# A transformer block on one core: its plan rebuilt with a longer time for the row sums' trip to DRAM, and the normalised h transposed by a DMA

## The chip, the cores and the metric

The kernel runs on one core of one Trainium2 chip. The metric is device time in microseconds (us), as the median of several executions. Engines are named as the profile names them: PE is TensorE (matmuls), PEld its weight loads, DVE is VectorE, ACT is ScalarE, POOL is GpSimd, SPq is the DMA queue that SyncE feeds.

## The reference

x has 2048 tokens of width 1024. There are 32 heads of width 32 that share one key and one value, and a feed-forward part of width 3584. All arrays are bf16.

```python
h  = x + attention(layernorm(x)) @ wo           # softmax over all 2048 keys
h2 = h + (sigmoid(n @ w_gate) * (n @ w_up)) @ w_down,   n = layernorm(h)
```

## The kernel before

The kernel is a small scheduler. It walks through the work once on the host with a formula for the duration of each operation, writes an ordered list of instructions for each engine, and then emits the lists with semaphore waits. The formula never runs on the chip: it only decides the order. Each engine then executes its list in that order, so an operation whose input is late holds up what is listed behind it: in the first trip shown below DVE stood idle 3.29 us before one multiplication, and the additions and the eviction listed behind it began only after it.

The formula for a DMA, in the planner's step:

```python
go = max(s + 1300.0, self.dma_free)
self.dma_free = go + o.nbytes / self.DMA_RATE      # DMA_RATE = 260 bytes per ns
o.end = self.dma_free + 700.0
```

Attention works on half tiles: 128 tokens and 16 heads, called hf. PE makes scores S_ps for one block of 128 keys, ACT makes the exponentials (Pr<-S_ps), DVE adds them up (acc<-acc,Pr). PE multiplies Pr with the values in two groups (PV), which DVE collects in the single buffer oun. After the last block PE adds acc over the partitions (SUM), and the reciprocals of the sums must reach all partitions. They make a trip through DRAM:

```python
rc = pl.op("dve", lambda: DVE.reciprocal(r_sb[:, :], F_ps[:, b, 0:64]), ...)
rd_ld[hf] = dma(lambda: SP.dma_start(r_dram, r_sb[0:P:4, :]), "rd", 8192, [rc, ...], prio=0)
rb_ld[hf] = dma(lambda: SP.dma_start(
    rb[:, :], bass.AP(r_dram.tensor, r_dram.offset, [[512, 4], [0, DH], [1, 512]])),
    "rb", 262144, [rd_ld[hf], ot_ev.get(hf - 1)], prio=0)
...
ot_ev[hf] = pl.op("dve", lambda: DVE.tensor_tensor(out=OT[...], in0=oun, in1=rb, op=ALU.mult),
    [oun_ev[(hf, 1)], op_last.get(c - 1), rb_ld[hf]], prio=0, occ=600, lat=690)   # abridged
```

OT then goes through wo (OP), h is normalised into hn, and hn is transposed for the feed-forward part by eight PE transposes into a PSUM bank and one DVE copy:

```python
def mk_hT(t):
    def atoms(b):
        tp = F_ps[:, b, :].bitcast(BF16)
        return [(lambda dt=dt: PE.transpose(out=tp[:, dt * P:(dt + 1) * P], in_=hn[:, dt * P:(dt + 1) * P],
                                            identity=ident[:, :]), P, "dense", []) for dt in range(DT)]
    def after(b, last):
        hT_last[t] = last
        hT_ev[t] = pl.op("dve", lambda: DVE.tensor_copy(out=hnT[:, :, t % 2, :], in_=src), ...)
```

PSUM is split: six banks hold scores, and two banks (F_ps) serve all other matmul groups. The feed-forward part of a tile (gate and up projections, hact, then the down projection) fills PE's time while ACT makes exponentials of later tiles.

The softmax here doesn't subtract the row's maximum and nothing guards it: scores larger than these inputs give would overflow.

## Time and profile before

| | before |
|---|---|
| median | 1211.61 us (3 runs, 1210.0 to 1219.1) |
| span of the profiled run | 1210.4 us |
| idle time of PE | 99.5 us (span less busy time) |
| DVE's wait for rb | 66.6 us, all 32 half tiles |

The first part of the page of the kernel before gives busy time, share of the span and instructions:

```profile
span 1210.4 us, 34593 instructions
...
PE 1110.9 (92%) x15144; PEld 757.5 (63%) x15176; DVE 869.1 (72%) x1076; ACT 1036.2 (86%) x1159; POOL 51.2 (4%) x93
```

The windows view of the kernel before gives busy time per stretch (start and end, length, then engines in the order PE, PEld, DVE, ACT, POOL, then granted clock, DMA share and GB/s). The stretch is from the middle:

```profile
400.00:800.00 400.00, 377.44 (x5386) 261.86 (x5390) 294.47 (x340) 380.57 (x421) 13.88 (x18) 1.00 0.58 177
```

PE and ACT are both near 95% there. The page also shows that 32 matmul records are missing (15144 matmuls for 15176 weight loads); their time counts as idle.

The waits view of PE in the kernel before (who waited for whom, us in all, times, longest), its largest entries in the attention stage:

```profile
PE F_ps L367 <- DVE hact L884: 24.5, 26, 3.0
PE F_ps L367 <- DVE oun L672: 17.6, 17, 2.8
PE S_ps L367 <- ACT Pr L601: 12.8, 22, 1.1
...
PE F_ps L367 <- DVE OT L652: 6.4, 3, 2.5
```

From the waits view over all engines, same kernel, one line of DVE and one of ACT:

```profile
DVE OT L652 <- DMA rb<-r_scratch: 66.6, 32, 6.8
...
ACT Pr L601 <- PE S_ps L367: 55.6, 58, 4.1
```

Read together: DVE stands before the OT multiplication until rb lands. PE waits for evictions that are listed on DVE behind it. ACT waits 55.6 us for scores that PE gives late. The chain that ended last, by line, says the same:

```profile
PE F_ps L367 44%; DMA rb<-r_scratch 13%; ACT Pr L601 8%; PE S_ps L367 8%; DVE acc L578 7%; DMA r_scratch<-r_sb 3%; DVE hact L884 2%; DVE oun L672 1%; DVE st L311 1%; SPq L825 1%; DVE st L313 1%; ACT tnh L878 1%; DVE r_sb L636 1%; PE F_ps L755 0%; DVE OT L652 0%
```

One trip in the timeline of the kernel before (start, length, engine, operation, in brackets the idle time before it and what ended it):

```profile
411.42 0.56 DVE L636 RECIPROCAL r_sb<-F_ps 128x64 f32<-128x64 f32 x1
...
412.01 0.49 SPq L638 DMA_DIRECT2D r_scratch<-r_sb  x1
...
415.08 0.55 SPq L639 DMA_DIRECT2D rb<-r_scratch  x1
...
420.50 0.69 DVE L652 TENSOR_TENSOR OT<-oun,rb 128x512 bf16<-128x512 f32 x1 [3.29 <-DMA rb<-r_scratch]
...
423.57 0.68 DVE L884 SCALAR_TENSOR_TENSOR hact<-tnh,F_ps 128x512 bf16<-128x512 f32 x1
...
424.31 0.65 PE L367 MATMUL F_ps<-hnT,ring 128*128 128x128 bf16 x8 [2.03 <-DVE hact L884]
```

The reciprocal ends at 411.98 and OT starts at 420.50: 8.5 us, where the formula gives about 5 us (2.0 for the write and 3.0 for the read). DVE idles 3.29 us, the eviction hact is late, and PE idles 2.03 us.

### The profile page before, as it was taken

The page shows a single profiled execution, that of the slowest core. Times are in us where ns is not written, and L with a number is a line of the kernel's source. Part 1 is how long each engine was busy: PE and PEld are TensorE (multiplying, and loading weights), DVE is VectorE, ACT ScalarE, POOL GpSimd, SP SyncE. Part 2 cuts the span into 40 slices and gives each one's busy share as a digit, 9 for nine tenths or more (in the row PEclk, how much of TensorE's full clock was granted, in tenths as well). Part 3 has the DMA queues.
Part 4 walks back from the last instruction along what each step waited for, and adds up shares of the span by engine and source line. Part 5 has one row for each costly group of instructions (what it writes and reads, how often), then busy time and mean ns, then how long its engine had stood idle before and what let it go on. Part 6 is the DMA issues. An engine that isn't in the chain of part 4 may idle for free.

```text
span 1210.4 us, 34593 instructions
## 1 busy us (share of the span) xinstructions
PE 1110.9 (92%) x15144; PEld 757.5 (63%) x15176; DVE 869.1 (72%) x1076; ACT 1036.2 (86%) x1159; POOL 51.2 (4%) x93
## 2 busy tenths in 40 slices
PE   6898978889999999999999999989999999999998
PEld 5533455557566665666666675657665675766797
DVE  8996878667786768687786768677776667777321
ACT  3899999889998999999998999989998998999110
POOL 3200000010000100010000100000000000000000
PEclk9899999999999999999999999999999999999999
DMA  9334284774747375664737384655747374664884
GB/s 314 118 96 150 84 263 138 228 228 149 219 129 213 103 230 150 182 197 138 238 115 228 102 251 142 203 171 165 216 134 221 94 214 131 191 192 123 240 261 128
DMA packets 213335, 214.47 MB, mean 177 GB/s; under 512 B 16192, under 2 KB 199488, under 8 KB 213184
## 3 DMA queue, kind: packets, MB, share of 16 engines
q1 hardware_dynamic: 213184, 212.26, 57.8%
q8 instruction: 119, 1.95, 0.7%
q14 instruction: 32, 0.26, 0.1%
HBM read 204.08 MB, written 8.13 MB: 175 GB/s over the span
## 4 chain that ended last, share of the span: by engine, by line
PE 53%; DMA 17%; DVE 14%; ACT 9%; issue 6%; SPq 1%; DVEq 0%
PE F_ps L367 44%; DMA rb<-r_scratch 13%; ACT Pr L601 8%; PE S_ps L367 8%; DVE acc L578 7%; DMA r_scratch<-r_sb 3%; DVE hact L884 2%; DVE oun L672 1%; DVE st L311 1%; SPq L825 1%; DVE st L313 1%; ACT tnh L878 1%; DVE r_sb L636 1%; PE F_ps L755 0%; DVE OT L652 0%
## 5 line engine op out<-in xcount | busy, mean ns | idle before, releaser
L601 ACT ACTIVATE Pr<-S_ps 128x1024 bf16<-128x1024 f32 x1008 | 965.5, 1034 | 63.2 <-PE S_ps L367 55.6
L578 DVE TENSOR_TENSOR acc<-acc,Pr 128x2048 bf16<-128x2048 bf16 x430 | 525.4, 1222 | 49.9 <-ACT Pr L601 30.7
L367 PE MATMUL F_ps<-hnT,ring 128*128 128x128 bf16 x6752 | 438.9, 220 | 21.9 <-DVE hact L884 8.7
L367 PEld LDWEIGHTS F_ps<-hnT,ring 128*128 128x128 bf16 x6752 | 385.1, 98 | 91.4 <-issue 65.5
L367 PE MATMUL F_ps<-zone,hact 128*128 128x256 bf16 x1792 | 225.8, 273 | 3.0 <-DVE hact L884 2.0
L367 PE MATMUL S_ps<-QTb,kT 32*128 32x512 bf16 x2048 | 204.2, 389 | 15.9 <-ACT Pr L601 12.8
L367 PEld LDWEIGHTS F_ps<-zone,hact 128*128 128x128 bf16 x1792 | 163.7, 98 | 47.8 <-issue 22.8
L367 PE MATMUL F_ps<-Pr,Vt 128*32 128x512 bf16 x2016 | 130.2, 387 | 5.7 <-DVE hact L884 5.5
L878 ACT ACTIVATE tnh<-F_ps 128x512 f32<-128x512 f32 x112 | 67.3, 601 | 71.9 <-PE F_ps L367 63.7
L367 PEld LDWEIGHTS S_ps<-QTb,kT 32*128 32x128 bf16 x2048 | 51.6, 91 | 121.4 <-ACT Pr L601 51.1
L884 DVE SCALAR_TENSOR_TENSOR hact<-tnh,F_ps 128x512 bf16<-128x512 f32 x112 | 76.4, 682 | 39.8 <-PE F_ps L367 36.6
L367 PE MATMUL F_ps<-wo_sb,OT 128*128 128x512 bf16 x234 | 67.1, 416 | 28.1 <-DVE hact L884 7.9
L367 PEld LDWEIGHTS F_ps<-Pr,Vt 128*32 128x32 bf16 x2016 | 46.5, 97 | 64.4 <-issue 21.6
L367 PE MATMUL F_ps<-zone 128*128 128x512 bf16 (+3 forms) x574 | 76.5, 282 | 7.1 <-DVE oun L672 2.8
L676 DVE TENSOR_TENSOR oun<-F_ps,oun 128x512 f32<-128x512 f32 x31 | 21.4, 691 | 75.3 <-PE F_ps L367 75.3
L652 DVE TENSOR_TENSOR OT<-oun,rb 128x512 bf16<-128x512 f32 x31 | 21.5, 693 | 65.4 <-DMA rb<-r_scratch 65.4
L367 PEld LDWEIGHTS F_ps<-zone 128*128 128x128 bf16 x584 | 41.2, 102 | 34.3 <-issue 8.3
L367 PEld LDWEIGHTS F_ps<-wo_sb,OT 128*128 128x128 bf16 x256 | 22.6, 103 | 60.7 <-issue 17.8
L324 POOL TENSOR_SCALAR zb<-mvb 128x1 bf16<-128x1 bf16 (+2 forms) x24 | 12.3, 511 | 1092.5 <-DVE mvb L320 1092.4
L920 DVE SCALAR_TENSOR_TENSOR h_sb<-F_ps,h_sb 128x256 bf16<-128x256 f32 x64 | 26.8, 419 | 25.4 <-PE F_ps L367 25.0
L636 DVE RECIPROCAL r_sb<-F_ps 128x64 f32<-128x64 f32 x32 | 17.8, 558 | 26.3 <-PE F_ps L367 26.3
L578 DVE TENSOR_TENSOR acc<-Pr 128x2048 bf16<-128x2048 bf16 x31 | 36.0, 1163 | 0.0
(70 smaller groups left out, 369.5 us busy)
## 6 DMA issues: line engine op xcount, KB each, us to landing
ring<-in_B_w_gate_dram SPq DMA_DIRECT2D x308, 256.0 KB, 3.8
ring<-in_B_w_up_dram SPq DMA_DIRECT2D x308, 256.0 KB, 3.6
rb<-r_scratch SPq DMA_DIRECT2D x32, 256.0 KB
zone<-in_B_w_down_dram SPq DMA_DIRECT2D x14, 512.0 KB, 4.8
Pr<-in_B_w_up_dram SPq DMA_DIRECT2D x20, 256.0 KB, 4.2
Pr<-in_B_w_gate_dram SPq DMA_DIRECT2D x20, 256.0 KB, 4.7
ring<-in_A_x_dram SPq DMA_DIRECT2D x16, 256.0 KB, 6.1
h_sb<-in_A_x_dram SPq DMA_DIRECT2D x16, 256.0 KB, 3.0
```

Of the source, the lines that this page charges most:

```text
L311: a = pl.op("dve", lambda s=s, src=src: DVE.bn_stats(st[:, s, 0, :], src[:, 0:512]), dp, prio=prio, occ=600, lat=756, order=[st_user.get(s)])
L313: b = pl.op("dve", lambda s=s, src=src: DVE.bn_stats(st[:, s, 1, :], src[:, 512:1024]), dp, prio=prio, occ=600, lat=756, order=[st_user.ge ...
L324: f = pl.op("pool", lambda: POOL.tensor_scalar(out=zb[:, ph, tk], in0=mvb[:, ph, tk, 1], scalar1=LN_EPS_BF16, scalar2=None, op0=ALU.add), ...
L367: return lambda: PE.matmul(o, lhsT=l, rhs=r, start=start, stop=stop, **kw)
L578: add_op[(hf, kt)] = pl.op("dve", lambda: DVE.tensor_tensor(out=a, in0=in0, in1=slot, op=ALU.add), dp, prio=6, **t_dve(2048, 1.92))
L601: exps[u] = pl.op("act", lambda i=i, pb=pb: ACT.activation(out=slot[:, i * 1024:(i + 1) * 1024].rearrange("p (a b) -> p a b", a=2), in_=S_ ...
L636: rc = pl.op("dve", lambda: DVE.reciprocal(r_sb[:, :], F_ps[:, b, 0:64]), [last, rd_ld.get(hf - 1)], prio=0, occ=64 * 8 / 0.96 + 20, lat=6 ...
L652: ot_ev[hf] = pl.op("dve", lambda: DVE.tensor_tensor(out=OT[:, 4 * hh:4 * hh + 4, :], in0=o.rearrange("p (a b) -> p a b", a=4), in1=rb[:, ...
L676: oun_ev[(hf, 1)] = pl.op("dve", lambda: DVE.tensor_tensor(out=o, in0=F_ps[:, b, :], in1=o, op=ALU.add), [last, oun_ev[(hf, 0)]], prio=0, ...
L878: box["a"] = pl.op("act", lambda: ACT.activation(out=tnh[:, :], in_=F_ps[:, b, :], func=ACTF.Tanh, scale=0.5), [last, box.get("e", ot_ev[1 ...
L884: e = pl.op("dve", lambda: DVE.scalar_tensor_tensor(out=ho, in0=shape(tnh[:, :]), scalar=1.0, in1=shape(F_ps[:, b, :]), op0=ALU.add, op1=A ...
L920: e = pl.op("dve", lambda: DVE.scalar_tensor_tensor(out=h_sb[:, t % 4, sl], in0=F_ps[:, b, 0:DW], scalar=0.5, in1=h_sb[:, t % 4, sl], op0= ...
```

## The change

It does two things. First, the plan adds a fixed lateness to the landing of four kinds of DMA, so that DVE gets other work ahead of the OT multiplication. Second, the transpose of hn leaves PE, PSUM and DVE, and becomes a DMA from SBUF to SBUF (DMA_TRANSPOSE in the trace, called crossbar transpose in the recorded texts). The diff, cut to its core:

```diff
+    LATE = {"rd": 1500.0, "rb": 3500.0, "hT0": 1000.0, "hT1": 1000.0}
...
-            o.end = self.dma_free + 700.0
+            o.end = self.dma_free + 700.0 + self.LATE.get(o.key, 0.0)
...
-                    queues["hT"].append(mk_hT(t))
+                    load_hT(t)
...
-        def mk_hT(t):                  # eight PE.transpose, one DVE.tensor_copy
...
+        def load_hT(t):
+            if t not in hnorm or t in hT_ev or (t >= 2 and (t - 2) not in gu_last):
+                return
+            hT_ev[t] = hT_last[t] = dma(lambda: SP.dma_start_transpose(hnT[:, :, t % 2, :], hn[:, :]), f"hT{t % 2}", P * D * 2,
+                                        [hnorm[t], gu_last.get(t - 2)] + (extra_rel if t < 2 else []), prio=0)
...
                         gu_last[t] = last
+                        load_hT(t + 2)
```

Both parts change the plan, so the order of nearly everything changes.

More of the change, by code (lines that the diff above doesn't have):

```diff
@@ L750, in mk_OP @@
             return Group("OP", atoms, lambda: [ot_ev[2 * t], ot_ev[2 * t + 1], wo_ld], after, gate)
-        def mk_hT(t):
-            def atoms(b):
-                tp = F_ps[:, b, :].bitcast(BF16)
-                return [(lambda dt=dt: PE.transpose(out=tp[:, dt * P:(dt + 1) * P], in_=hn[:, dt * P:(dt + 1) * P],
-                                                    identity=ident[:, :]), P, "dense", []) for dt in range(DT)]
-            def after(b, last):
-                hT_last[t] = last
-                src = F_ps[:, b, :].bitcast(BF16).rearrange("p (a b) -> p a b", a=DT)
-                hT_ev[t] = pl.op("dve", lambda: DVE.tensor_copy(out=hnT[:, :, t % 2, :], in_=src),
-                                 [last, gu_last.get(t - 2)] + (extra_rel if t < 2 else []), prio=1, **t_dve(1024, 1.92))
-                return [hT_ev[t]]
-            return Group("hT", atoms, lambda: [hnorm[t]], after, lambda: t < 2 or (t - 2) in gu_last)
+        def load_hT(t):
[3 more added lines that the diff above has]
+                                        [hnorm[t], gu_last.get(t - 2)] + (extra_rel if t < 2 else []), prio=0)
         ffn_next = [0]
```

## The prediction

> **What bounds the kernel now.** The page gives PE 1110.9 us busy of a 1210.4 us span (92%), ACT 1036.2 (86%), DVE 869.1 (72%). The windows view splits it: from 400 to 800 us PE is busy 377 and ACT 381 of 400, so two engines are near full and neither has room; from 1130 us on ACT is done and PE runs the last tile alone. What remains is some 99 us of PE idle time. By the waits view of PE, about 55 us of it end with a DVE operation (hact 24.5, oun 17.6, OT 6.4, four more about 7), 13 us with an exponential. The waits view of DVE says why DVE is late: before all 32 multiplications OT<-oun,rb it stands still for rb<-r_scratch, 66.6 us in all (0.5 to 6.8 each). DVE works in order, so the PSUM evictions behind it wait, and PE with them. The chain agrees: 13% on rb, 3% on r_scratch. In the timeline a trip from reciprocal to landed rb takes 7.5 us (second half of a tile) to 11.8 us (first half); the plan's formula gave it about 5.
>
> **What the change does.**
> 1. The plan now gives the trip about 10 us. DVE gets additions and evictions ahead of the OT multiplication. Adding up the PE stalls of over 0.6 us that follow an rb wait in the timeline, I get about 50 us (1 to 3 us each). Not all comes back: oun is one buffer, so the first PV group of the next half holds one of two PSUM banks until OT is done, in the first halves.
> 2. 128 TensorE transposes go: 10.3 us of PE. Sixteen DVE copies go: 11.1 us of DVE plus 16.4 us that it waited for them.
> 3. Sixteen crossbar transposes of 256 KB come, planned at about 4 us each. [...] plain 256 KB loads here land in 3.0 to 3.8 us. No trace of mine shows a transpose yet; I expect 3.5 to 6 us. PE is covered meanwhile by down projections and scores, except a few us before the last tile.
>
> **On the critical path.** Upper bound: 50 + 10 = 60 us. In the attention stage PE needs about 910 and ACT about 918 of 990 us; both cannot be over some 96% full together, so I count half: about 30 us, mostly from step 1 (22), the rest from step 2 (9), less 2 for the last tile's transpose.
>
> **Predicted: 1182 us, 8 in 10 between 1158 and 1212.** Faster by over 2%: 0.58; within 2%: 0.31; slower by over 2%: 0.11.
>
> **What would show it.** Step 1: DVE's wait for rb falls from 66.6 to under 20 us, PE's waits for hact, oun and OT from 48 to about 25, and rb leaves the chain's first places. Step 2: PE busy falls to about 1100. Step 3: transposes land in under 6 us, PE waits for hnT stay under 10 us, and loads of weights still land in about 4 us. ACT in 400 to 800 us is over 96% busy.
>
> **What would make it wrong.** Transposes of 8 us or more, or queued behind weight loads: PE, in order, would stand still up to 5 us for each of 16 tiles (80 us). A transpose stuck at the head of SP's queue that holds back weights. A rebuilt order that is worse elsewhere by chance, or a longer planned hold of the bank, giving back what the waits lose. Tiles falling into pairs, which changes the order altogether.

## The result

| | before | after |
|---|---|---|
| median | 1212.76 us (the 3 runs above and one more, 1210.0 to 1219.1) | 1160.01 us (4 runs, 1159.69 to 1160.09) |
| ratio | | 0.9557, 95% interval 0.9519 to 0.9596 |
| idle time of PE | 99.5 us | 69.4 us |
| DVE's wait for rb | 66.6 us | 0.8 us |
| end of the last exponential | 1123.1 us | 1062.6 us |

A ratio here and below is the mean time of one kernel's runs over that of the kernel before in the same rounds, so it is not quite the ratio of the medians quoted.

The same lines of the kernel after, first the page:

```profile
span 1157.9 us, 34384 instructions
...
PE 1088.5 (94%) x15022; PEld 745.1 (64%) x15048; DVE 859.1 (74%) x1057; ACT 1033.8 (89%) x1162; POOL 41.7 (4%) x93
```

The windows view of the kernel after, the same stretch:

```profile
400.00:800.00 400.00, 384.66 (x5474) 263.94 (x5469) 306.17 (x350) 394.50 (x439) 8.00 (x18) 1.00 0.62 184
```

ACT is now busy 98.6% of it. The waits view of PE in the kernel after:

```profile
PE S_ps L368 <- ACT Pr L602: 13.7, 20, 1.4
PE F_ps L368 <- DVE oun L673: 9.8, 14, 1.7
...
PE F_ps L368 <- DVE r_sb L637: 7.4, 15, 0.6
PE F_ps L368 <- DVE h_sb L915: 5.8, 9, 0.9
...
PE F_ps L368 <- DVE hact L878: 2.9, 5, 0.8
```

The waits view of DVE in the kernel after:

```profile
DVE OT L653 <- DMA rb<-r_scratch: 0.8, 2, 0.5
```

The waits view of ACT in the kernel after:

```profile
ACT Pr L602 <- PE S_ps L368: 5.9, 20, 1.6
```

PE's waits for hact, oun and OT fell from 48.5 to 12.7 us, and ACT's for scores from 55.6 to 5.9. Some waits of PE grew: for r_sb from 1.0 to 7.4 us and for h_sb (L920 before, L915 after) from 2.8 to 5.8. In the chain of the kernel after, rb has 1% where it had 13%:

```profile
PE F_ps L368 66%; PE S_ps L368 12%; ACT Pr L602 6%; DVE acc L579 5%; DVE st L312 1%; DVE r_sb L637 1%; DVE st L314 1%; DVE oun L673 1%; DMA rb<-r_scratch 1%; DVE zone L253 1%; DVE zone L351 1%; DVE ring L344 1%; DMA ring<-in_B_w_up_dram 0%; ACT tnh L872 0%; DVE hact L878 0%
```

A trip in the timeline of the kernel after:

```profile
614.04 0.56 DVE L637 RECIPROCAL r_sb<-F_ps 128x64 f32<-128x64 f32 x1 [0.76 <-PE F_ps L368]
...
614.63 0.49 SPq L639 DMA_DIRECT2D r_scratch<-r_sb  x1
...
619.59 0.56 SPq L640 DMA_DIRECT2D rb<-r_scratch  x1
...
625.75 0.69 DVE L878 SCALAR_TENSOR_TENSOR hact<-tnh,F_ps 128x512 bf16<-128x512 f32 x1 [0.68 <-PE F_ps L368]
...
627.57 0.68 DVE L653 TENSOR_TENSOR OT<-oun,rb 128x512 bf16<-128x512 f32 x1
```

The OT multiplication comes 13.0 us after the reciprocal, later than in the example of before, but DVE evicts hact ahead of it and no longer stands still for rb. The trip itself did not get shorter: counted in the packed traces from its issue to the last update of its semaphore, rb lands after 6.2 us in the median in both kernels.

The tile view of hnT in the kernel after shows the new DMA: its length on the SP queue (shortest, median, longest, ns), and the time from issue to landing:

```profile
L757 SPq DMA_TRANSPOSE hnT<-hn x16: 1262/1293/1584, 141.7 to 1091.9; - x16
...
DMA to landing us min/median/max: 3.1/4.3/5.0
```

Plain loads of the same 256 KB landed in 2.7 to 6.1 us in the kernel after (medians by tile in its DMA view), those of weights into ring in 3.8 and 3.9. On the SP queue the plain DMAs of the row sums took 0.49 us (write) and 0.57 us (rb) in the median, where a transpose took 1.29.

**Where the 52.5 us of the spans went.** By stage: the last exponential ends 60.5 us sooner, and the stretch after it, where PE finishes alone, became 8.1 us longer (87.2 to 95.3). By PE's account: idle time fell by 30.1 us and busy time by 22.4. The transposes explain 10.3 us of the busy time. The rest, 12.1 us, is of the size of what the clock costs less.

The windows view of the kernel before around the stall shown above, in steps of 1 us; the granted clock is the third number from the right:

```profile
423.00:424.00 1.00, 0.00 (x0) 0.00 (x0) 1.00 (x2) 0.00 (x0) 0.00 (x0) 1.00 0.46 93
424.00:425.00 1.00, 0.69 (x12) 0.56 (x12) 1.00 (x2) 0.60 (x1) 0.00 (x0) 0.89 1.03 358
425.00:426.00 1.00, 1.00 (x10) 0.56 (x7) 0.90 (x2) 0.44 (x1) 0.00 (x0) 0.50 0.30 95
426.00:427.00 1.00, 1.00 (x14) 0.80 (x15) 0.90 (x2) 1.00 (x2) 0.00 (x0) 0.50 0.77 225
427.00:428.00 1.00, 1.00 (x13) 0.39 (x16) 1.00 (x1) 0.49 (x1) 0.00 (x0) 0.50 0.45 82
428.00:429.00 1.00, 1.00 (x16) 0.22 (x12) 0.90 (x2) 0.05 (x1) 0.00 (x0) 0.91 0.70 221
```

PE stood still from 422.3 to 424.3, and then it had half its clock for over 3 us while it was busy. This stall was so paid twice. The profiled run of before has eleven such episodes after the first 20 us, and nine of them follow a PE stall of 1.9 to 3.1 us. The kernel after has two. These two (at 146 and 166 us), and the other two of before (at 45 and 52 us), follow several shorter stalls, none of them over 1.5 us. So one long stall is not the only way into half clock. Nor did every long stall lead there: three others of before, of 2.8, 2.1 and 2.7 us (they end at 119.6, 326.2 and 661.9 us), were followed by full clock, so no limit on the length of a single stall sorts the cases seen here. Each of the episodes, eleven before and two after, lasted 3.41 us at a granted clock of 0.50; what starts one is not shown. Summing (1 - clock) times PE's busy time over the steps gives 17.8 us lost before and 3.0 after. e1, which keeps the transposes on PE, fits this: it loses 4.5 us, and its busy time is 12.9 us below that of before.

### The profile page after: what moved, and what is told of

Its sections match the earlier page's. It is cut to its first block, busy times and chain, and to the rows that moved or that the text cites. A ratio compares the mean times of both kernels' runs of the same rounds, so it can differ in the third digit from the quotient of the medians.

```text
span 1157.9 us, 34384 instructions
## 1 busy us (share of the span) xinstructions
PE 1088.5 (94%) x15022; PEld 745.1 (64%) x15048; DVE 859.1 (74%) x1057; ACT 1033.8 (89%) x1162; POOL 41.7 (4%) x93
## 4 chain that ended last, share of the span: by engine, by line
PE 77%; DVE 11%; ACT 6%; issue 4%; DMA 1%; SPq 0%; POOL 0%; DVEq 0%
PE F_ps L368 66%; PE S_ps L368 12%; ACT Pr L602 6%; DVE acc L579 5%; DVE st L312 1%; DVE r_sb L637 1%; DVE st L314 1%; DVE oun L673 1%; DMA rb<-r_scratch 1%; DVE zone L253 1%; DVE zone L351 1%; DVE ring L344 1%; DMA ring<-in_B_w_up_dram 0%; ACT tnh L872 0%; DVE hact L878 0%
## 5 line engine op out<-in xcount | busy, mean ns | idle before, releaser
L368 PE MATMUL F_ps<-zone,hact 128*128 128x256 bf16 x1792 | 228.3, 273 | 3.0 <-DVE hact L878 1.9
L368 PE MATMUL F_ps<-zone 128*128 128x512 bf16 (+3 forms) x574 | 73.7, 274 | 6.4 <-DVE zone L253 2.1
L368 PE MATMUL F_ps<-wo_sb,OT 128*128 128x512 bf16 x240 | 59.8, 380 | 4.1 <-DVE oun L673 2.0
L915 DVE SCALAR_TENSOR_TENSOR h_sb<-F_ps,h_sb 128x256 bf16<-128x256 f32 x64 | 26.9, 420 | 49.4 <-PE F_ps L368 49.3
L637 DVE RECIPROCAL r_sb<-F_ps 128x64 f32<-128x64 f32 x32 | 17.8, 557 | 50.4 <-PE F_ps L368 50.4
L325 POOL TENSOR_SCALAR zb<-mvb 128x1 bf16<-128x1 bf16 (+2 forms) x24 | 6.4, 267 | 1043.0 <-DVE mvb L321 1042.8
L736 DVE TENSOR_TENSOR h_sb<-F_ps,h_sb 128x512 bf16<-128x512 f32 x32 | 22.0, 686 | 10.1 <-PE F_ps L368 9.6
```

Of the source, the lines that this page charges most:

```text
L368: return lambda: PE.matmul(o, lhsT=l, rhs=r, start=start, stop=stop, **kw)
L736: h_ev[(t, dc)] = pl.op("dve", lambda: DVE.tensor_tensor(out=h_sb[:, t % 4, sl], in0=F_ps[:, b, :], in1=h_sb[:, t % 4, sl], op=ALU.add), [ ...
L915: e = pl.op("dve", lambda: DVE.scalar_tensor_tensor(out=h_sb[:, t % 4, sl], in0=F_ps[:, b, 0:DW], scalar=0.5, in1=h_sb[:, t % 4, sl], op0= ...
```

## The experiments

Theory W: the gain is DVE no longer standing still for rb; through DVE's order this stalled PE, and through PE it stalled ACT. Rival T: most of it comes from taking the transposes off PE and the copies off DVE. Rival L: any rebuilt plan can fall better or worse by several per cent, and the longer trip is only one way to rebuild it. Every run below was correct unless it is said. This table collects them. DVE's wait, ACT's wait and the two stages are of the profiled run of each kernel; the tail is the span after the last exponential. The groups ran on three different chips, in three sessions, with before at 1211.8 us in the first (e1 to e4), 1204.6 in the second (e5 to e8) and 1203.9 in the third (e9 to e12), so across groups the ratios are to be compared. e4, a single look, and e6, whose result is wrong, are told in the text alone.

| run | median us | ratio to before (95%) | DVE waits for rb | ACT waits for scores | last exp ends | tail |
|---|---|---|---|---|---|---|
| before | | 1 | 66.6 | 55.6 | 1123.1 | 87.2 |
| after | 1160.0 | 0.956 (0.952 to 0.960) | 0.8 | 5.9 | 1062.6 | 95.3 |
| e1 longer trip only | 1164.9 | 0.963 (0.958 to 0.968) | 0.9 | 7.2 | 1061.2 | 101.1 |
| e2 transposes only | 1199.9 | 0.991 (0.984 to 0.998) | 48.0 | 53.3 | 1111.2 | 93.2 |
| e3 no wait, old order | 1152.3 | 0.953 (0.947 to 0.959) | 0 | 8.5 | 1066.0 | 86.2 |
| e5 half of the longer trip | 1168.8 | 0.970 (0.966 to 0.974) | 9.4 | 24.7 | 1082.8 | 85.5 |
| e7 other rebuild | 1219.4 | 1.012 (1.007 to 1.017) | 58.8 | 66.9 | 1122.5 | 97.5 |
| e8 trip really shorter, old order | 1150.7 | 0.955 (0.952 to 0.959) | 11.4 | 9.6 | 1064.3 | 84.6 |
| e9 transposes, e8's trip, short plan | 1158.6 | 0.961 (0.956 to 0.965) | 4.3 | 8.8 | 1065.1 | 91.0 |
| e10 the same, plan to fit | 1149.8 | 0.953 (0.948 to 0.959) | 3.1 | 11.5 | 1069.5 | 82.0 |
| e11 after, e8's trip | 1160.4 | 0.963 (0.958 to 0.967) | 0 | 6.2 | 1063.6 | 95.0 |
| e12 after again | 1159.9 | 0.962 (0.957 to 0.966) | 1.0 | 5.6 | 1062.3 | 94.8 |

### e1: the longer trip alone

```diff
# kernel before
+    LATE = {"rd": 1500.0, "rb": 3500.0}
-            o.end = self.dma_free + 700.0
+            o.end = self.dma_free + 700.0 + self.LATE.get(o.key, 0.0)
```

> The kernel before with the longer trip in its plan, and nothing else: the transposes stay on TensorE. Theory W (the gain is DVE no longer standing still before the OT multiplication): DVE's wait for rb falls from 66.6 us to under 5 us, PE's waits for hact, oun and OT from 48 to under 20 us, time 1165 to 1178 us (ratio about 0.965). Rival T (taking the transposes off TensorE and the copies off DVE brings most): time above 1190 us. Rival L (any rebuilt plan can fall well or badly): anything, with no relation to the waits.

Measured: ratio 0.963. The waits view of DVE in e1:

```profile
DVE OT L653 <- DMA rb<-r_scratch: 0.9, 2, 0.7
```

PE's waits for the main hact, oun and OT lines fell to under 9 us. Most of the change's gain is here, without any DMA transpose. T falls as the main cause.

### e2: the DMA transposes alone

```diff
# kernel after
-    LATE = {"rd": 1500.0, "rb": 3500.0, "hT0": 1000.0, "hT1": 1000.0}
+    LATE = {"hT0": 1000.0, "hT1": 1000.0}
```

> The changed kernel with the old, short trip of the row sums in its plan: only the crossbar transposes. Theory W: DVE still waits 50 us or more for rb, PE is busy some 10 us less than before, time 1198 to 1207 us (ratio about 0.99). Rival T: time below 1185 us. Rival L: anything.

Measured: ratio 0.991, inside the range of W. The wait for rb was 48.0 us, a little under the 50 expected. 0.963 times 0.991 is 0.954, and the whole change measured 0.956, or 0.962 in e12; each ratio is known to about half a per cent, so this agrees with adding up but does not show it. PE's busy time fell by only 3.2 us (1107.7), where some 10 had been expected, and DVE's wait for rb fell by 18.6. So it is not shown that the 0.9% comes from the transposes. Later runs show that the parts do not always add up.

### e3: the wait taken away, the order kept

```diff
# kernel before, cut to its core; the planner still plans with rb, the emitter leaves that one wait out
-                in1=rb[:, :].rearrange("p (a b) -> p a b", a=4), op=ALU.mult),
+                in1=kT4[:, 0:512].rearrange("p (a b) -> p a b", a=4), op=ALU.mult),
+            ot_ev[hf].soft = rb_ld[hf]
-                    if d.eng == e and e == "pe":
+                    if (d.eng == e and e == "pe") or d is o.soft:
```

> The kernel before, the same order of instructions on every engine, but the OT multiplication reads a constant tile instead of rb, so that DVE does not wait for the trip (the result is wrong on purpose; the trip itself still runs). Theory W: as good as the longer trip in the plan or a little better, 1160 to 1175 us, and PE's waits for hact, oun and OT fall from 48 to under 15 us. Rival L (the gain is in the new order, not in the wait): within 1% of before, 1200 to 1215 us. Rival T: also above 1190 us.

The constant tile is a part of the keys, which is written once, early; SyncE waits for the last trip at the end of the program. The result was wrong. I compared the lists of the two kernels: the order is the same on every engine. Measured: ratio 0.953, with 1152.3 us faster than W's range. The waits of PE for DVE and of ACT for scores in e3:

```profile
PE F_ps L368 <- DVE hact L886: 4.8, 13, 2.4
...
PE F_ps L368 <- DVE oun L674: 2.1, 7, 0.4
```

```profile
ACT Pr L602 <- PE S_ps L368: 8.5, 22, 2.3
```

With not one instruction moved, the whole gain is there, so L falls as the explanation: it is the wait. Its wrong values are no rival, since e8 below gains as much in the same order with the right ones. The part of the clock shows here as well. The profiled run lost 7.7 us to half clock by the sum above, against 17.8 before.

### e4: an edit that left the order as it was

```diff
# kernel before
+    LATE = {"xr0": 1500.0, "xr1": 1500.0, "xr2": 1500.0, "xr3": 1500.0}
# and the line of o.end as in e1
```

> Placeholder control: the kernel before with a longer planned landing for another load, that of x for the residual; the order of instructions comes out the same on every engine, so all theories expect the time of before within 0.5%. It gives the granted clock of an identical program once more: if the clock of the profiled run of before (0.984) belongs to that run and not to the program, it should differ here.

This was one look: 1207.7 us and a mean clock of 0.993, where the profiled run of before had 0.984. The same sum of lost PE time gives 8.2 us, against 17.8 for the identical order. Its longest stall after the start, 3.3 us before 1002.2 us, was followed by full clock. So not every long stall costs the clock, and the clock's part of the gain is between about 5 and 15 us of PE time, an estimate from these sums (8.2 and 17.8, less the 3.0 of after), by chance of the run. The executions of before say the same: in the first session 1202.4 us went with a clock of 0.993, and 1211.8 us with 0.983.

### e5 and e6: half and twice the lateness

```diff
# e1
-    LATE = {"rd": 1500.0, "rb": 3500.0}
+    LATE = {"rd": 750.0, "rb": 1750.0}      # e5
+    LATE = {"rd": 3000.0, "rb": 7000.0}     # e6
```

> The kernel before, TensorE transposes, with half of the longer trip in its plan (750 and 1750 ns). Theory W (the gain follows what DVE still waits for rb): some 20 to 30 us of DVE wait for rb remain, time between before and the full value, 1175 to 1195 us. Theory C (part of the gain is the TensorE clock, which the trace shows at 0.50 for some 3.4 us after PE stalls of 2 us and more): stalls become shorter than 2 us, so half-clock episodes vanish although waits remain, and the granted clock is 0.993 or more. Rival L (luck of a rebuilt order): no relation.

Measured in e5: ratio 0.970 (1168.8 us), between before and e1 but faster than the range expected. The wait that remained (9.4 us) is less than expected: half of the lateness already covers 23 of the 32 trips. The gain does not follow this wait alone. e8 below leaves about as much of it (11.4 us) and gains 4.5%, where e5 gains 3.0%; in e5, a rebuilt order, PE also waits 12.9 us for h_sb and ACT 24.7 us for scores. Theory C failed in its detail: the profiled run has seven episodes of half clock and its executions ran at 0.988 to 0.994. Short remaining waits for rb did not save it from other stalls.

> The same with twice the longer trip (3000 and 7000 ns). Theory W: no wait for rb is left, as in the run with the full value (1164.9 us); what is added is a later OT, which holds oun and one PSUM bank longer: 1165 to 1185 us. Rival L: no relation.

Measured in e6: 1233.4 us, ratio 1.024, and a wrong result (relative error 0.26). W had expected 1165 to 1185 us, so this is a miss. There are two reasons in the trace. The first is the order: the timeline shows OP of a tile coming so late that four times two tiles were processed as a pair, and PE had 165 us of work left after the last exponential. The second is a lost dependency. In the timeline of e6:

```profile
995.63 0.68 DVE L653 TENSOR_TENSOR OT<-oun,rb 128x512 bf16<-128x512 f32 x1
...
1011.30 1.03 PE L368 MATMUL F_ps<-wo_sb,OT 128*128 128x512 bf16 x4
```

The next tile's first half is written into OT at 995.6, before the matmuls of the tile before have read it at 1011.3. The planner protects OT with `op_last.get(c - 1)`. This gives nothing, and so no dependency, when the reader has not been planned yet. In e6 the trace shows it once. e6 is therefore not a point on the curve of W.

### e7: another rebuild of the plan

```diff
# kernel before
-SWITCH = 97.0
+SWITCH = 107.0
```

> The kernel before with one unrelated constant of its plan changed (cost of a change of matmul mode 107 instead of 97 ns): the order of PE, DVE, ACT and SP comes out different, the trip is planned as short as before. Theory W: DVE still waits 50 us or more for rb and the time is within 1.5% of before. Rival L: a change of several per cent is as likely here as from the longer trip.

Measured: 1.2% slower, with 58.8 us of waits for rb. Its last exponential ends where that of before does (1122.5 and 1123.1), and its tail is 10 us longer. Both expectations of W held. So luck is real, about 1% large, and here it sits mostly in the tail; one sample does not bound it.

### e8: the trip made shorter instead of planned longer

The kernel before makes four equal copies of each reciprocal in neighbouring partitions and writes one of them. Here they are laid out so that all 128 rows go to DRAM, and the broadcast reads 16 rows eight times instead of 4 rows 32 times.

```diff
# kernel before
-            c_sel = pl.op("pool", lambda i=i: POOL.memset(sel[:, i, 4 * i:4 * i + 4], 1.0), [c_sel], occ=60)
+            c_sel = pl.op("pool", lambda i=i: POOL.memset(sel[:, i, i:DH:8], 1.0), [c_sel], occ=60)
-        r_dram = nc.dram_tensor("r_scratch", [32, 64], F32, kind="Internal").ap()
+        r_dram = nc.dram_tensor("r_scratch", [P, 64], F32, kind="Internal").ap()
-   SP.dma_start(r_dram, r_sb[0:P:4, :])
+   SP.dma_start(r_dram, r_sb[:, :])
-   [[512, 4], [0, DH], [1, 512]]
+   [[512, 16], [0, 8], [1, 512]]
```

> The kernel before with the trip really shortened instead of planned longer: the sums' broadcast reads its source with an outermost dimension of 16 instead of 4 (the four equal copies of each sum, which lay unused, are written to DRAM too); the plan's order is the same but for nothing. [...] rb lands some 2 us sooner than the 4.7 to 7 us of before, DVE's wait for rb falls from 66.6 us to 15 to 35 us, and by theory W the time is 1170 to 1195 us. If the landing time is all queueing behind weights, nothing changes (1205 to 1215 us).

Measured: 1150.7 us, ratio 0.955, and 11.4 us of waits for rb: more gain and less wait than W's ranges had. The order on the engines is again that of before. The tile view of rb in e8:

```profile
  DMA rb<-r_scratch: 11.4, 11
...
DMA to landing us min/median/max: 3.0/3.7/6.4
```

In before, where DVE stood waiting at nearly every trip, rb landed 4.6 to 9.0 us after its issue; here the median is 3.7. The 2 us expected were my estimate. The packed traces show one more difference: the semaphore of rb is updated 5 times for each transfer in before (160 for 32) and 16 times in e8 (512 for 32). With the same order on every engine, the wider pattern thus went with the shorter landing and with more updates, which queueing behind weights does not explain; why it lands sooner is not shown. So a correct kernel with the old plan, TensorE transposes and an rb that lands 2.5 us sooner (medians 6.2 and 3.7) gains as much as the whole change. This is the third way of taking the same wait away, after e1 and e3, with the same result.

### e9 to e12: the parts together, and a version faster than both

```diff
# e9 and e10: kernel after with the four edits of e8
-    LATE = {"rd": 1500.0, "rb": 3500.0, "hT0": 1000.0, "hT1": 1000.0}
+    LATE = {"hT0": 1000.0, "hT1": 1000.0}                               # e9
+    LATE = {"rd": 750.0, "rb": 750.0, "hT0": 1000.0, "hT1": 1000.0}     # e10
# e11: kernel after with the four edits of e8 alone.   e12: kernel after, unchanged
```

> Crossbar transposes with the old, short trip in the plan (the order of the run with the transposes alone), and the broadcast read with 16 as the outermost dimension. If the two savings add as they did in the change (0.9554 for the wide broadcast, 0.9909 for the transposes alone), the ratio is 0.947 (about 1142 us at 1206 us before), better than the changed kernel. If both only remove the same PE stalls, it stays at 0.955.

> The same with a trip in the plan that fits the wide broadcast (750 ns longer for each of its two DMAs instead of 1500 and 3500). The 11.4 us that DVE still waited for rb with the wide broadcast should go to under 3 us: ratio 0.942 to 0.950. The other rebuild of the plan moved the time by 1.2%, so the order alone can shift this by about as much.

> The changed kernel, its plan and order as they are, with the wide broadcast. DVE no longer waits for rb in it, so by theory W a sooner landing has nothing left to save: within 0.5% of the changed kernel. Rival B (the narrow broadcast also slows the loads of weights and the time comes from there): faster than the changed kernel by 1% or more.

> The changed kernel again, on the same chip as the three others, for a direct comparison: ratio to before 0.952 to 0.960 as in the first result.

e11 and e12 agree within 0.1% (0.963 and 0.962). For e12 a ratio of 0.952 to 0.960 had been expected, so 0.962 lies just outside; its own median is that of the first result within 0.2 us. A faster trip gains nothing where DVE no longer waits for it: this is the counter-test of W, and it speaks against a gain through the loads of weights.

e9 failed its first expectation of 0.947, and at 0.961 it is no better than e8's 0.955. Taking the transposes off PE went with 0.9% in e2 and with at most 0.7% between e1 and the change (0.963 against 0.956, or 0.962 in e12; the intervals overlap), and here it brought nothing or a loss. The windows view says where to look, with e8 first and e9 second; each line is the attention stage to its last exponential:

```profile
50.00:1064.30 1014.30, 979.76 (x13588) 653.40 (x13620) 801.81 (x925) 998.63 (x1108) 31.42 (x45) 1.00 0.59 182
```

```profile
50.00:1065.10 1015.10, 977.88 (x13394) 642.71 (x13392) 792.75 (x908) 997.02 (x1104) 27.86 (x45) 1.00 0.62 183
```

Both stages have the same length, and ACT is busy over 98% of both. Work taken off PE cannot shorten a stage that ACT now sets; it could only shorten the tail, and the tail is 91.0 us in e9 and 84.6 in e8. The waits view of PE in e9 shows one new cost, against 1.0 us in e8:

```profile
PE F_ps L368 <- DVE r_sb L637: 12.1, 21, 0.7
```

In e9 and in e2, which have the same order on all engines but for one DMA's form, PE waits 21 times for the reciprocal that frees the bank of the sums. The lines view shows a second one: the matmuls of the gate and up projections (F_ps<-hnT,ring and F_ps<-hnT,Pr, 7168 in each kernel) are busy 474.2 us in e9 and 459.2 in e8, 15 us more, and 481.2 in e2 against 464.2 in before. The PE time of the two lines above is not quite like with like, since e8 lacks 32 matmul records there and e9 none. That these two costs use up the 10 us of the transposes is argued from the sizes; why this order stretches the projections is open.

e10 was the fastest correct kernel of the third session, though its ratio of 0.953 and its 3.1 us of waits for rb just missed what was expected (0.942 to 0.950, under 3): 1149.8 us (1148.6 to 1153.3) against 1159.9 (1158.9 to 1160.2) for the changed kernel on the same chip, 0.9% less. It and e8 beat both kernels; between them there is nothing to choose. Their advantage over the changed kernel lies in a tail 10 to 13 us shorter, and the attention stage is not shorter at all.

## Why the prediction was right or wrong

The time (1160.0 us) fell inside the range of 1158 to 1212, but only 2 us above its lower end. The direction and the mechanism were right, and the size of the gain was off: about 30 us expected, 52.8 by the medians.

- **What bounds the kernel, and step 1: right.** DVE's wait for rb fell from 66.6 to 0.8 us, where under 20 was expected. PE's waits for hact, oun and OT fell from 48.5 to 12.7, where about 25 was expected. Four runs that take most or all of the wait away by different means (e1, e3, e5, e8) gain 3 to 4.7%; two that leave 48 us or more of it (e2, e7) gain 0.9% and lose 1.2%. Inside the first group the gain does not follow the wait that is left (9.4 us in e5, 11.4 in e8), so the order counts there too.
- **The failed step is "both cannot be over some 96% full together, so I count half", an estimate of mine that no trace had shown.** In the stretch from 400 to 800 us ACT went from 95% to 98.6%, with PE at 96.2%. I had read two engines at 94 to 95% as two limits. They had one common cause of idle time. The last exponential came 60.5 us sooner; that this is near the upper bound of 60 us is chance, since the bound was a sum of PE time. By PE's account the 52.5 us are 30.1 of idle time, 10.3 of transposes and 12.1 of other busy time, where the prediction had 22, 9 and nothing. So the halving cost the forecast about 8 us, and the missing term that follows about 12.
- **A term was missing: the clock.** PE's busy time was expected to fall to about 1100 us and fell to 1088.5 (1092.7 in e12, where no record is missing). Half clock, in nine of eleven episodes of 3.41 us after a stall of 1.9 to 3.1 us, had cost 17.8 us of PE time in the profiled run of before and cost 3.0 after (8.2 in e4, another run of the order of before).
- **Another term was missing: the tail.** It grew from 87.2 to 95.3 us. The prediction had 2 us there for the last transpose. The whole 8 us are of the size by which another rebuilt order moves the tail (10 us in e7). Each part alone lengthens it as well (101.1 us in e1, 93.2 in e2), and e3 and e8, whose exponentials end as early in the old order, do not (86.2 and 84.6). So it belongs to these rebuilt orders and is not the transposes' alone; what in them causes it is open.
- **The hold of one PSUM bank** while OT waits was named as a loss. PE's waits for oun stayed at 9.8 us of 17.6, so it is small. Nor does it show as the reason why e8, which keeps OT early, ends sooner than e1: the attention stage of e1 ends 3.1 us before that of e8, and the tail of e1 is 16.5 us longer.
- **Step 2 was half right.** The transposes went (10.3 us of PE, 11.1 of DVE). The time that went with them was 0.9% alone, at most 0.7% with the longer trip, and nothing with the shorter trip. The 9 us of the sum were near the 11 us of e2, but that kernel also waited 18.6 us less for rb and PE's busy time hardly fell, so this may be luck.
- **Step 3: right.** The 3.0 to 3.8 us that the prediction gives for plain loads of 256 KB are those of weights into ring and of x for the residual; others took longer in before (medians of 4.2 to 6.1 us for Pr<-in_B and ring<-in_A_x). The transposes landed in 3.1 to 5.0 us, where I had estimated 3.5 to 6, the waits view of PE has no wait for hnT (its one wait for a DMA is 0.2 us, for ring), and weights still landed in 3.8 to 3.9 us.

## What to carry to other kernels

A planned order is only as good as the latencies in it: one underestimated DMA (planned at about 5 us with its write, 8.5 us in the trip shown) at the head of an engine's list idled two other engines, although the engine that waited was the least busy of the three (72%, against 86 and 92%). Before planning around a latency, see whether it can be shortened; a wider access pattern did here what the whole change did. When two engines are both at 95%, look for a common stall before calling either the limit, count what a stall does to the clock (17.8 us of PE time in the profiled run of before), and check by a run with the wait removed and the order kept.
